# An FFT feeding a routed expert layer: loads, folds and the opening chain put in another order

## The chip, the cores and the metric

One core of a Trainium2 chip runs the whole program. The metric is the time of one execution on the device in microseconds (us), lower is better. A comparison gives the median of several executions of each kernel on the same chip.

## What is computed

```python
X = np.fft.fft(x, axis=1)          # x: 8 batches x 2496 rows x 256 columns
X = np.fft.fft(X, axis=2)
x = X.real.reshape(8 * 2496, 256)  # 19968 tokens
logits = x @ w_gate                # 8 experts
expert_idx = np.argmax(logits, axis=1)
gate_w = softmax(logits)[arange, expert_idx]
for e in range(8):                 # w1: 256 x 1024, w2: 1024 x 256
    out[mask_e] = gate_w[mask_e] * (relu(x[mask_e] @ w1[e]) @ w2[e])
```

## The kernel before

The work has two halves that overlap. The first half makes tokens: 16 units, each half of one batch's outputs (unit 2b is the even half of batch b, unit 2b+1 the odd half). The second half is the expert layer ("MoE"), which takes tokens of one expert in groups of 256 or 512 rows.

**Tokens.** A batch's rows arrive in the tile x, in four quarters and five slots of 128 rows. DVE folds them (`fold_w`, `fold_fg`, `fold_z`, `fold_h`, or `fold_half` for batch 1), so that symmetric rows are added and subtracted. TensorE then multiplies by cosine and sine tables cs0 (even half) and cs1 (odd half): `along_s(u, q)`, written (u, q) from here on, two chains of products per unit (q = 0 and 1), each ending in two PSUM banks; `s_out` copies one with ACT (tile ec) and lets DVE add and subtract into the tile pc or qc. `along_d(u)` multiplies five blocks of 128 columns by the tables in pack, ACT copies each result (tile pl) and DVE adds it into the unit's rows rb. `route_a` and `route_b` find each row's expert on DVE (lg, mx, ls, oh, mn, ohf, sm, then sc, rp, dst, di) and ACT (ex, sm, ohb); in their middle stand two small TensorE products with the triangle trib and the tile ones, which count the rows of each expert before a row. The result di is the row's place. `send` has GpSimd (POOL) scatter the unit's rows to the bucket in device memory, 10 indirect DMAs for a unit.

Column 0 of the second transform is a plain sum over all columns, which is made apart: `g1_fold` folds the tile xg on POOL, `g1_sums(par)` multiplies it by the tables, and `g1_rows(par, g1)` turns the 8 x 625 result so that it can be added to the rows (tile g1t).

**MoE.** When 2, 4, 7, 12 and 16 units are done, `group_table` makes a table on DVE that says which expert and which rows each of the next groups takes; SyncE (SP) loads it (`fetch`, tile row), reads registers from it, and loads weights (w1r, w2r) and rows (xr, L801). The first groups can only be loaded when the 20 scatters of units 0 and 1 have landed. A group then has its rows turned on TensorE (`xpose`, L852), split into a high and a low part (xh on ACT, xl on DVE), multiplied by split weights (wah, wal; L885 to L887), passed through relu (hh, hl), multiplied by the second weights (wb; L911, L912) and scattered to out.

**What sets the order.** Each engine runs its own instructions in the order in which they were built. The recorder places an instruction by readiness, and `with stage(engines)` ties all of a block's instructions on the named engines behind those of the block before. The opening (units 0 and 1 entire) is written out by hand in `fft_steps` as such blocks. From unit 2 on, the token work is a generator whose steps are taken a few at a time beside the steps of `moe_steps`; PRE of them are taken before the first MoE step.

The diff touches the opening's loads (L260 to L273), `stage`, `g1_sums`, `g1_rows`, `gate_weights`, `fold_first`, `route_a`, `along_d`, `fft_steps`, `xpose`, `gemm1` and `moe_steps`.

Of the kernel before, what the change touches and what calls it, by code (L numbers as in the profile page):

```python
# [21 lines left out]
P = 128  # L22
# [12 lines left out]
FSTEPS, PRE = (15, 26), 15  # L35
# [5 lines left out]
KEPT = 4  # L41
NE = NK * 2
# [152 lines left out]
def fft2_then_moe(ctx: ExitStack, tc: tile.TileContext, i: dict, out: bass.AP):  # L195
# [30 lines left out]
    def stage(*engines):  # L226
# [5 lines left out]
        for e in engines:  # L232
            mine = [q for q in traced[first:] if q.engine == e]
            for q in mine:
                for before in behind.get(e, ()):
# [3 lines left out]
            if mine:  # L239
                behind[e] = [q.name for q in mine]  # L240
# [27 lines left out]
    for t, n in ((pack, "c_pack"), (cdl, "c_cdl"), (wg, "wg"), (wgl, "wgl")):  # L268
        nc.sync.dma_start(out=t, in_=i[n])
    nc.sync.dma_start(out=cs0[:, 1], in_=i["c_cs0"][:, 1])  # L270
    load_x(1)
    nc.sync.dma_start(out=cs1[:, 1], in_=i["c_cs1"][:, 1])
    nc.sync.dma_start(out=ids, in_=i["c_ids"].rearrange("p (b n) -> p b n", b=B))  # L273
# [92 lines left out]
    def g1_sums(par):  # L366
        g1 = ff.tile([P, NKK], F32, name="pc")
        pe, po = bank("S"), bank("S")
        s_mm(pe, po, gz[:, par], gzs, par, B)
        ec = ff.tile([P, M], F32, name="ec")  # L370
        eo = ff.tile([P, M], F32, name="ec")
        nc.scalar.copy(ec[0:B], pe[0:B, 0:M])
        nc.scalar.copy(eo[0:B], po[0:B, 0:M])
        nc.gpsimd.tensor_add(g1[0:B, 0:M], ec[0:B], eo[0:B])
        nc.gpsimd.tensor_sub(g1[0:B, M : 2 * M - 1], ec[0:B, 0 : M - 1], eo[0:B, 0 : M - 1])
        return g1

    def g1_rows(par, g1):
# [11 lines left out]
    def gate_weights():  # L390
        nc.vector.tensor_copy(trib, tri)
        nc.vector.tensor_copy(tacc[:, 2:3], io[:, 2:3])
        nc.vector.tensor_add(wsum, wg[:, 0:E], wg[:, E : 2 * E])
        nc.vector.tensor_sub(wdif, wg[:, 0:E], wg[:, E : 2 * E])
        gp = bank("R")
# [75 lines left out]
    def fold_first():  # L471

        for sl in slots:
            yield from fold_w(0, sl)
            yield from fold_fg(0, sl)
            yield from fold_z(0, 0, sl, (0,))
            if sl is slots[1]:
                yield from fold_h(0, (0, 1))
# [99 lines left out]
    def fft_steps():  # L578
# [47 lines left out]
        with stage(PE, DVE):  # L626
            gate_weights()
# [453 lines left out]
```

## Time and profile before

| | us |
|---|---|
| median of 3 runs | 1107.19 |
| lowest, highest | 1101.07, 1109.17 |
| the profiled execution | 1100.43 |
| span of its instructions | 1098.4 |

The profile is of one execution. Its span goes from the first instruction to the last; 2.0 us of the execution's time lie around it. PE is TensorE's matmuls, PEld its weight loads, DVE is VectorE, ACT is ScalarE. A product of 32-bit operands has two records in the trace. PEclk is the granted TensorE clock as a share of full speed: 1.00 is 2.4 GHz, 0.50 is 1.2 GHz.

### The profile page before, as it was taken

Reading aid. Unit: us, or ns where it says so; the run is one execution under the profiler, and the core shown is the slowest. Engines: PE = TensorE matmul, PEld = TensorE weight load, DVE = VectorE, ACT = ScalarE, POOL = GpSimd, SP = SyncE. Lnnn points to the kernel's source line nnn. Section 1 sums busy time; section 2 is a strip of 40 time slices with the busy share of each in tenths; the row PEclk is TensorE's granted clock in tenths of the full one; section 3 lists DMA queues with packets and bytes.
Section 4 is the critical chain, followed back from the end, with each engine's and each line's share of the span. In section 5 each row is a group of like instructions: output and inputs, shape, how many; then the busy total and the mean of one; then the engine's idle time right before and its main releaser. Section 6 shows DMA issues by size and latency. Waiting matters only on the chain.

```text
span 1098.4 us, 19262 instructions
## 1 busy us (share of the span) xinstructions
PE 1071.3 (98%) x5840; PEld 897.1 (82%) x5840; DVE 817.3 (74%) x1819; ACT 582.3 (53%) x1330; POOL 358.9 (33%) x355
## 2 busy tenths in 40 slices
PE   8679999999999999999999999999999999999997
PEld 4459888898978878888887888888888888888896
DVE  6879997978897797976766776666766666666664
ACT  1347665566655545555555555555554455555554
POOL 2445433165155444533152552111211122111212
PEclk9679999999999999999999999999999999999999
DMA  9468667367886647655454556644564456544445
GB/s 366 171 225 296 231 228 265 119 223 223 278 219 198 212 110 238 173 158 154 116 164 121 160 172 173 165 116 116 166 159 137 116 149 159 154 116 128 161 175 195
DMA packets 185677, 197.88 MB, mean 180 GB/s; under 512 B 155515, under 2 KB 156316, under 8 KB 170844
## 3 DMA queue, kind: packets, MB, share of 16 engines
q1 hardware_dynamic: 170108, 154.06, 47.7%
q0 software_dynamic: 15456, 42.50, 10.3%
q8 instruction: 48, 0.79, 0.3%
q14 instruction: 65, 0.53, 0.1%
HBM read 154.03 MB, written 45.20 MB: 181 GB/s over the span
## 4 chain that ended last, share of the span: by engine, by line
PE 89%; issue 5%; DVE 2%; POOL 2%; DMA 2%; POOLq 0%; ACT 0%; SPq 0%; DVEq 0%; ACTq 0%
PE psY L911 26%; PE psH L885 13%; PE psY L912 13%; PE psH L886 13%; PE psH L887 13%; PE psH L318 6%; PE psH L598 2%; PE psH L599 1%; POOL bucket L549 1%; PE psY L318 1%; DMA x<-xin 1%; POOL out L920 1%; PE psH L852 1%; DMA bucket<-rb,di 0%; DMA xr<-bucket 0%
## 5 line engine op out<-in xcount | busy, mean ns | idle before, releaser
L911 PE MATMUL psY<-wb,hh 128*128 128x512 f32 x1296 | 474.4, 400 | 0.0
L912 PE MATMUL psY<-wb,hl 128*128 128x256 f32 x1296 | 363.1, 280 | 0.0
L920 POOL DMA_INDIRECT out<-ys,gt x162 | 170.4, 1052 | 539.1 <-DVE ys L919 502.3
L911 PEld LDWEIGHTS psY<-wb,hh 128*128 128x128 f32 x1296 | 243.5, 188 | 55.9 <-issue 2.2
L885 PE MATMUL psH<-xh,wah 128*128 128x512 f32 (+1 forms) x768 | 281.8, 367 | 0.7 <-ACT xh L854 0.7
L886 PE MATMUL psH<-xl,wah 128*128 128x512 f32 (+1 forms) x768 | 276.8, 360 | 0.2 <-DVE xl L855 0.2
L887 PE MATMUL psH<-xh,wal 128*128 128x512 f32 (+1 forms) x768 | 274.4, 357 | 0.0
L892 DVE SCALAR_TENSOR_TENSOR hl<-psH,hh 128x512 fp32r<-128x512 f32 x324 | 222.0, 685 | 47.3 <-ACT hh L891 43.5
L912 PEld LDWEIGHTS psY<-wb,hl 128*128 128x128 f32 x1296 | 244.6, 189 | 9.0
L861 DVE TENSOR_TENSOR wal<-w1r,wah 128x512 fp32r<-128x512 f32 x192 | 132.4, 690 | 153.7 <-ACT wah L860 150.1
L860 ACT CAST wah<-w1r 128x512 fp32r<-128x512 f32 x192 | 119.1, 621 | 213.7 <-PE psH L886 211.5
L891 ACT ACTIVATE hh<-psH 128x512 fp32r<-128x512 f32 x324 | 192.8, 595 | 65.6 <-PE psH L887 62.7
L549 POOL DMA_INDIRECT bucket<-rb,di x160 | 176.0, 1100 | 146.1 <-PE psH L887 59.7
L885 PEld LDWEIGHTS psH<-xh,wah 128*128 128x128 f32 x768 | 145.0, 189 | 29.3 <-issue 1.8
L887 PEld LDWEIGHTS psH<-xh,wal 128*128 128x128 f32 x768 | 145.5, 189 | 23.1
L886 PEld LDWEIGHTS psH<-xl,wah 128*128 128x128 f32 x768 | 145.5, 189 | 11.5 <-DVE xl L855 0.4
L871 ACT CAST wb<-w2r 128x512 fp32r<-128x512 f32 x192 | 119.9, 626 | 65.1 <-PE psY L912 61.7
L872 DVE TENSOR_TENSOR wb<-w2r,wb 128x512 fp32r<-128x512 f32 x192 | 130.8, 682 | 26.3 <-ACT wb L871 25.8
L854 ACT CAST xh<-psH 128x512 fp32r<-128x512 f32 x81 | 47.6, 590 | 46.7 <-DVE psH L848 45.1
L318 PE MATMUL psH<-cs,x 128*128 128x313 f32 (+3 forms) x336 | 71.7, 414 | 0.0
L919 DVE SCALAR_TENSOR_TENSOR ys<-psY,gt,ys 128x256 f32<-128x256 f32 x162 | 67.7, 474 | 3.2 <-ACT ys L918 3.2
L918 ACT ACTIVATE ys<-psY,gt 128x256 f32<-128x256 f32 x162 | 65.7, 481 | 4.3 <-PE psY L912 3.4
(144 smaller groups left out, 738.0 us busy)
## 6 DMA issues: line engine op xcount, KB each, us to landing
w1r<-w SPq DMA_DIRECT2D x50, 1024.0 KB, 5.4
w2r<-w SPq DMA_DIRECT2D x50, 1024.0 KB, 5.4
x<-xin SPq DMA_DIRECT2D x14, 1280.0 KB, 9.1
xr<-bucket SPq DMA_DIRECT2D x248, 64.0 KB, 4.8
xr<-bucket SPq DMA_DIRECT2D x15, 266.0 KB, 4.8
out<-ys,gt POOLq DMA_INDIRECT x162, 4.7
bucket<-rb,di POOLq DMA_INDIRECT x160, 4.5
bucket<-c_pad SPq DMA_DIRECT2D x8, 266.0 KB, 8.4
```

What stands on the lines that cost most here:

```text
L318: mm = lambda *a, **k: ch.update(pe=nc.tensor.matmul(*a, **k).ins)
L549: ins = nc.gpsimd.indirect_dma_start(out=bucket[:, :], out_offset=IndirectOffsetOnAxis(ap=di[:, n : n + 1].bitcast(U32), axis=0), in_=rb[: ...
L861: nc.vector.tensor_sub(lo, src, hi.bitcast(F32))
L872: nc.vector.tensor_sub(wb[:, :, 1], src, wb[:, :, 0].bitcast(F32))
L885: nc.tensor.matmul(o, lhsT=wh[:, c], rhs=xh[:, k, :], start=(k == 0), stop=False)
L886: nc.tensor.matmul(o, lhsT=wh[:, c], rhs=xl[:, k, :], start=False, stop=False)
L887: ins = nc.tensor.matmul(o, lhsT=wl[:, c], rhs=xh[:, k, :], start=False, stop=(k == 1))
L891: nc.scalar.activation(hh, hp, AF.Relu)
L892: nc.vector.scalar_tensor_tensor(out=hl, in0=hp, scalar=0.0, in1=hh.bitcast(F32), op0=ALU.max, op1=ALU.subtract)
L911: nc.tensor.matmul(y, lhsT=hh[:, c], rhs=wide_w, start=(first and q == 0), stop=end, skip_group_check=True)
L912: nc.tensor.matmul(y[:, 0:D], lhsT=hl[:, c], rhs=wb[:, f, 0], start=False, stop=end, skip_group_check=True)
L920: ins = nc.gpsimd.indirect_dma_start(out=out, out_offset=IndirectOffsetOnAxis(ap=gt[:, a, 1:2].bitcast(U32), axis=0), in_=ys, in_offset=No ...
```

## The change

Five things are done. The loads of the opening stand in another order. DVE folds batch 1 behind the first table, instead of during units 0 and 1, and the folds of batches 2 and 6, which stood beside units 3 and 11, now stand at units 4 and 12, behind the tables that follow units 3 and 11 (batch 2's also behind a named instruction of the second MoE group, `hold`). `g1_rows` adds column 0's two partial sums on TensorE: ten products that accumulate in pairs take the place of five transposes, POOL's adds go, and ACT makes four copies a half instead of two. `g1_sums(1)` and `g1_rows(1)` move from the start of the opening behind `along_d(0)`. The stages of the opening now tie PE, ACT and DVE, not mostly DVE alone. Smaller edits: the gate columns of a group are copied after its rows are turned, the copy of 127 columns in rb stands behind lg, seven of the eight pad loads come later, and the pace of the token steps is counted by `fft_work`.

```diff
     load_x0(slots[0])
     nc.sync.dma_start(out=xg, in_=i["xg"])
+    load_x0(slots[1])
     nc.sync.dma_start(out=cs0[:, 0], in_=i["c_cs0"][:, 0])
-    load_x0(slots[1])
-    nc.sync.dma_start(out=cs1[:, 0], in_=i["c_cs1"][:, 0])
     load_x0(slots[2])
...
     def g1_sums(par):
-        g1 = ff.tile([P, NKK], F32, name="pc")
         pe, po = bank("S"), bank("S")
         s_mm(pe, po, gz[:, par], gzs, par, B)
...
+        eo = []
+        for o, sign in ((pe, 1.0), (po, -1.0)):
+            t = ff.tile([P, NKK], F32, name="pc" if o is pe else "qc")
+            nc.scalar.copy(t[0:B, 0:M], o[0:B, 0:M])
+            nc.scalar.mul(t[0:B, M : 2 * M - 1], o[0:B, 0 : M - 1], sign)
+            eo.append(t)
+        return eo
...
         for kt in range(NK):
-            nc.tensor.transpose(out=gp[:, kt * B : (kt + 1) * B], in_=g1[0:B, KO[kt] : KO[kt] + P], identity=ident[0:B, 0:B])
+            for n, t in enumerate(eo):
+                nc.tensor.matmul(
+                    gp[:, kt * B : (kt + 1) * B], lhsT=t[0:B, KO[kt] : KO[kt] + P], rhs=ident[0:B, 0:B], start=(n == 0), stop=(n == 1)
+                )
...
-        g2 = g1_sums(1)
         with stage(PE, DVE):
-            run(fold_first())
+            for sl in slots:
+                run(fold_first(sl))
             along_s(0, 0, False)
         with stage(PE, DVE):
+            gate_sums()
+            run(fold_z(0, 1))
+            along_s(0, 1, False)
+        with stage(PE, ACT, DVE):
+            along_s_out(0, 0)
             gate_weights()
...
             g1_rows(0, g1)
...
             gate_g1(0)
...
+        with stage(PE, ACT, DVE):
             along_s_out(0, 1)
+            along_s(1, 0, False)
+        with stage(PE, ACT, DVE):
+            run(along_d(0))
+            g1 = g1_sums(1)
+            g1_rows(1, g1)
+            along_s(1, 1, False)
+        st, rb = {}, cols.pop(0)
+        with stage(ACT, DVE):
+            nc.vector.tensor_copy(trib, tri)
+            run(route_a(0, 0, rb, st))
+            along_s_out(1, 0)
             gate_g1(1)
...
+            along_s_out(1, 1)
+        with stage(PE, ACT, DVE):
             run(route_b(0, 0, rb, st))
             send()
...
+        load_x(2)
         ch["done"] = 2 if SEGS[0][0] == 2 else 0
+        yield
+        for h in (0, 2):
+            run(fold_half(1, h))
+        run(fold_z(1, 0))
+        run(fold_h(1))
```

Three places show what this does to the engines' order. The first is TensorE between unit 0's last transform and its first route product, before: the odd half's second chain (1, 1) in the banks psY_351 and psY_352, and right behind it the product with trib.

```order
L599 MATMUL psH<-pack,qc 128x136
L318 MATMUL psY_351<-cs_71,x 128x313 x2
L318 MATMUL psY_352<-cs_71,x 128x313 x2
L318 MATMUL psY_351<-cs_71,x 128x313
L318 MATMUL psY_352<-cs_71,x 128x313
L520 LDWEIGHTS trib
L520 MATMUL psH<-ohb,trib 128x80
```

The same place in the changed kernel; gz is the folded column-0 input, and the two L382 rows stand for five such pairs.

```order
L601 MATMUL psH<-pack,qc 128x136
L319 MATMUL psY_299<-cs_71,gz 8x313 x2
L319 MATMUL psY_300<-cs_71,gz 8x313 x2
L319 MATMUL psY_299<-cs_71,gz 8x313
L319 MATMUL psY_300<-cs_71,gz 8x313
L382 MATMUL psH<-pack,pc 128x8
L382 MATMUL psH<-pack,qc 128x8
...
L319 MATMUL psY_326<-cs_71,x 128x313 x3
L319 MATMUL psY_327<-cs_71,x 128x313 x3
L522 LDWEIGHTS trib
L522 MATMUL psH<-ohb,trib 128x80
```

The odd half's sums of column 0 and the ten products that turn them now stand in front of (1, 1) and of the route product. The second place is DVE in the changed kernel, from the end of the first table (tab) on; x is batch 1's tile.

```order
L760 TENSOR_SCALAR tab<-tacc 128x1
L761 TENSOR_TENSOR tab<-tacc 128x1
L457 TENSOR_TENSOR x<-x 128x1280 x2
L459 TENSOR_TENSOR x<-x 128x5x128
L461 TENSOR_TENSOR x<-x 128x5x128
L459 TENSOR_TENSOR x<-x 128x5x128
L461 TENSOR_TENSOR x<-x 128x5x128
L435 TENSOR_TENSOR x<-x 128x5x128 x3
L446 TENSOR_TENSOR zs<-x 128x512
L435 TENSOR_TENSOR x<-x 128x5x128
L448 TENSOR_TENSOR x<-x 128x2x2x128
```

These twelve folds were spread over units 0 and 1 and are now in one block behind the table, in front of everything that unit 2 needs. The third place is TensorE around the first MoE group, before: unit 3's second chain (six products with cs_71) stands in front of the turn of the first rows (xr).

```order
L520 MATMUL psH<-ohb,trib 128x80
L521 LDWEIGHTS ones
L521 MATMUL psH<-ohb,ones 128x80
L318 MATMUL psH<-cs_71,x 128x313 x6
L852 MATMUL psH<-pack,xr 128x128 x4
L885 MATMUL psH<-xh,wah 128x256 x2
```

And in the changed kernel:

```order
L522 MATMUL psH<-ohb,trib 128x80
L523 LDWEIGHTS ones
L523 MATMUL psH<-ohb,ones 128x80
L847 MATMUL psH<-pack,xr 128x128 x4
L885 MATMUL psH<-xh,wah 128x256
L319 MATMUL psH<-cs_71,x 128x313 x3
L886 MATMUL psH<-xl,wah 128x256
```

The turn of the first rows still stands behind unit 2's route products, while unit 3's second chain moved behind it, among the first group's products.

## Rows read from the trace of the kernel before

**Rows 1.** The page, part 1: busy us (share of the span) and instructions.

```profile
PE 1071.3 (98%) x5840; PEld 897.1 (82%) x5840; DVE 817.3 (74%) x1819; ACT 582.3 (53%) x1330; POOL 358.9 (33%) x355
```

**Rows 2.** Stretches: us, PE, PEld, DVE, ACT, POOL busy (instructions), PEclk, DMA share, GB/s.

```profile
0.00:81.00 81.00, 61.20 (x272) 39.78 (x273) 61.51 (x182) 23.70 (x88) 30.46 (x41) 0.77 0.69 255
81.00:1091.00 1010.00, 1009.90 (x5570) 857.30 (x5569) 754.86 (x1636) 558.17 (x1241) 326.49 (x313) 1.00 0.58 175
8.00:12.00 4.00, 1.17 (x10) 0.41 (x10) 2.05 (x4) 0.00 (x0) 2.77 (x7) 1.00 1.03 399
...
48.80:59.60 10.80, 10.80 (x43) 8.26 (x43) 8.97 (x42) 1.07 (x3) 8.39 (x10) 0.50 0.28 100
...
76.90:80.10 3.20, 2.98 (x14) 2.90 (x14) 2.65 (x5) 0.36 (x1) 0.00 (x0) 0.50 1.00 392
116.00:160.00 44.00, 43.90 (x300) 37.73 (x299) 42.01 (x143) 27.10 (x70) 18.68 (x18) 1.00 0.63 223
```

**Rows 3.** Timeline of PE: start us, us, line, operation, out<-in, records.

```profile
17.39 0.80 PE L318 MATMUL psY<-cs,x 128*128 128x156 f32 x4
...
20.15 0.39 PE L396 MATMUL psH<-wsum,pack 128*128 128x8 f32 x2
...
21.42 0.80 PE L318 MATMUL psY<-cs,zs 128*128 128x156 f32 x4
...
23.81 0.78 PE L381 MATMUL psH<-pack,pc 8*128 8x8 f32 x10
...
26.49 1.20 PE L598 MATMUL psH<-pack,pc 128*128 128x137 f32 x8
...
30.90 3.00 PE L318 MATMUL psY<-cs,x 128*128 128x313 f32 x12
37.02 0.22 PE L520 MATMUL psH<-ohb,trib 128*128 128x80 bf16 x1 [3.12 <-ACT ohb L505]
...
48.73 0.23 PE L520 MATMUL psH<-ohb,trib 128*128 128x80 bf16 x1 [5.25 <-ACT ohb L505]
...
48.83 2.20 PE L318 MATMUL psH<-cs,x 128*128 128x156 f32 x8
...
57.46 1.74 PE L598 MATMUL psH<-pack,pc 128*128 128x137 f32 x6
...
67.70 5.86 PE L318 MATMUL psH<-cs,x 128*128 128x313 f32 x12
...
76.48 0.50 PE L885 MATMUL psH<-xh,wah 128*128 128x256 f32 x2 [0.67 <-ACT xh L854]
```

**Rows 4.** Timeline of PE's weight loads.

```profile
20.15 0.30 PEld L396 LDWEIGHTS psH<-wsum,pack 128*128 128x128 f32 x2 [0.17 <-issue]
```

**Rows 5.** Timeline of DVE.

```profile
23.07 1.48 DVE L455 TENSOR_TENSOR x<-x 128x1280 f32<-128x1280 f32 x1
...
25.65 0.82 DVE L457 TENSOR_TENSOR x<-x 128x640 f32<-128x640 f32 x1
...
39.30 0.17 DVE L538 TENSOR_TENSOR di<-dst,pack 128x10 int32<-128x10 f32 x1
...
46.72 0.23 DVE L485 TENSOR_TENSOR lg<-rb,gg 128x80 f32<-128x80 f32 x1
...
50.63 0.17 DVE L538 TENSOR_TENSOR di<-dst,pack 128x10 int32<-128x10 f32 x1
...
56.99 0.14 DVE L761 TENSOR_TENSOR tab<-tacc 128x1 int32<-128x1 f32 x1
...
63.91 0.24 DVE L485 TENSOR_TENSOR lg<-rb,gg 128x80 f32<-128x80 f32 x1
```

**Rows 6.** Timeline of POOL: the first and the last of units 0 and 1's 20 scatters.

```profile
40.41 1.54 POOL L549 DMA_INDIRECT bucket<-rb,di  x1 [5.10 <-DVE x L457]
...
66.63 0.98 POOL L549 DMA_INDIRECT bucket<-rb,di  x1 [0.30 <-issue]
```

**Rows 7.** The chain that ended last, in order of time: the first load of rows.

```profile
72.28 2.76 DMA xr<-bucket
```

More of the change, by code (lines that the diff above doesn't have):

```diff
@@ L234, in stage @@
             for q in mine:
-                for before in behind.get(e, ()):
+                for before in [since] if since else behind.get(e, ()):
                     tc.add_manual_dep(
@@ L238, in stage @@
                     )
-            if mine:
+            if mine and not since:
                 behind[e] = [q.name for q in mine]
@@ L648, in fft_steps @@
-        rest = fold_half(1, 2)
-        with stage(DVE):
-            run(along_d(0))
-            run(half)
-            next(rest)
-        st, rb = {}, cols.pop(0)
-        with stage(DVE):
-            along_s(1, 0)
-            run(route_a(0, 0, rb, st))
-        with stage(DVE):
-            along_s(1, 1)
+            along_s(1, 0, False)
[4 more added lines that the diff above has]
+            along_s(1, 1, False)
@@ L668, in fft_steps @@
-        with stage(DVE):
+        with stage(PE, ACT, DVE):
+            nc.vector.tensor_copy(tacc[:, 2:3], io[:, 2:3])
             run(route(1))
             send()
+        load_x(2)
+        ch["done"] = 2 if SEGS[0][0] == 2 else 0
         yield
-        ch["done"] = 2 if SEGS[0][0] == 2 else 0
+        for h in (0, 2):
+            run(fold_half(1, h))
+        run(fold_z(1, 0))
+        run(fold_h(1))
         late = None
@@ L678, in fft_steps @@
                 pads(range(1, E))
-            if par == 0 and b + 1 < B:
+            if par == 0 and 1 < b < B - 1:
                 load_x(b + 1)
+            if par == 0 and u in NS and u > 2:
+                folds = fold_batch(b)
+                while True:
+                    with stage(DVE, since=ch.get("hold")):
+                        if next(folds, 0) == 0:
+                            break
+                    yield
             if (u, 0) not in cols:
@@ L689, in fft_steps @@
                 yield from fold_z(b, 1)
-            elif b + 1 < B:
-                with tc.issue_after(ch["tab"]) if b == 1 else nullcontext():
-                    yield from fold_batch(b + 1)
+            elif b + 1 < B and u + 1 not in NS:
+                yield from fold_batch(b + 1)
             yield from along_d(u)
             late = route(u)
-            if u + 1 in [n for n, _, _ in SEGS]:
+            if u + 1 in NS:
                 if par == 0:
@@ L855, in xpose @@
         nc.vector.tensor_sub(xl, hp, xh.bitcast(F32))
+        if part == 0 and not blocked(g):
+            gt = mo.tile([P, 4, 2], F32, name="gt", bufs=8)
+            nc.scalar.copy(gt[:, 0:n, 0], xr[:, 0:n, GATE])
+            nc.vector.tensor_copy(gt[:, 0:n, 1].bitcast(I32), xr[:, 0:n, TID].bitcast(I32))
+            ch[g, "gt"] = gt
     def split(src, name):
@@ L995, in fft_until, with fft_work @@
             yield
+    def fft_work(u):
+        folds = 19 if (u + 1) // 2 <= EARLY else 13
+        if u % 2:
+            return 13 + folds * (u + 1 not in NS)
+        return 15 + folds * (u in NS and u > 2)
     segs = cuts()
@@ L1027, in fft2_then_moe @@
         todo = fft_until(n)
-        rate = sum(FSTEPS[u % 2] for u in range(was, n))
+        rate = sum(fft_work(u) for u in range(was, n))
         if made[-2] == 0:
@@ L1042, in fft2_then_moe @@
                 next(todo, None)
-            with nullcontext() if k else stage(ACT, DVE):
+            with stage(ACT, DVE) if k < 6 else nullcontext():
                 next(moe)
```

81 lines of the change are left out of this document (26 added, 55 removed).

## The prediction

> **What bounds the kernel now.** I read the page first: TensorE is busy 98% of the span [rows 1]. A table of stretches then says where the other 2% lie [rows 2]. From 81 to 1091 us PE is busy 1009.9 of 1010 us at the full clock: no stall is left there that an edit could remove, and whatever stands outside it adds to the time one for one. From 0 to 81 us it is busy 61.2 of 81 us, at 0.77 of the clock. So all the edits must be judged by two numbers: when the first MoE product starts, and how much token work TensorE has done by then, because work that is left over costs its full length later.
>
> Before, the first MoE product (L885) starts at 76.48 [rows 3]. It hangs on the scatters: unit 0's places di are ready at 39.47, the first of 20 scatters starts at 40.41 and the last at 66.63 [rows 5, 6]; SP can issue the load of rows at 72.28, it takes 2.76 us [rows 7], and turning and splitting takes the rest. In the shadow of the scatters TensorE does unit 2 entirely and both chains of unit 3; the last of these runs from 67.70 to 73.56 [rows 3].
>
> **The opening, step by step.** Start: cs0's first half (128x939 numbers, 0.48 MB) now stands behind the second third of x; at 399 GB/s [rows 2] that is 1.2 us for x. I let (0,0) start 1.0 us earlier, 16.4 instead of 17.39. From there TensorE is one queue. (0,0) and what waits in it took 17.39 to 20.15, 2.8 us; the gate products 20.15 to 21.42, 1.3; (0,1) 21.42 to 23.81, 2.4 [rows 3]. So 22.9 so far.
>
> New: ten products for column 0 in place of five transposes. Before, ten transposes (both halves) took 23.81 to 24.52, 0.07 us each [rows 3]. A 32-bit product with 8 columns is priced by the gate's four: 1.27/4 = 0.32 us each. From below, the two weight loads of one such product end 0.30 us after the first begins, and the row's x2 covers one load of about 0.19 after a step of about 0.11 [rows 4], so 0.23 us each if nothing else counts. I take 0.25, near the loads, since the ten have no waits between them: 2.5 us a half (ends: 0.7 at the transposes' price, 3.2). That gives 25.4. (1,0) costs 3.0 like the chain at 30.90 [rows 3]: 28.4. `along_d(0)`: eight records of L598 took 26.49 to 27.53 and the other factor's as much, so 0.52 a block, 2.6 for five: 31.0.
>
> Now the moved part. `g1_sums(1)` used to run while TensorE waited for x; here it stands in the queue. Its six products are as wide as the chain at 30.90, 3.0 us: 34.0. Two ACT copies must follow before the ten products, some 0.7 us: 34.7. The ten products: 37.2. (1,1): 40.2. Then comes the route product, at 40.2 instead of 37.02. What is given back is the 3.12 us in which PE waited for ohb [rows 3]: `route_a` now hides behind this queue, so that cover is worth all it can be and is used up. ACT runs in order too: ohb, unit 0's, stands behind the four copies and the g1t copy, about 38.5, still before 40.2.
>
> di of unit 0: 2.45 us behind the route product before (37.02 to 39.47), plus about 0.4 because the adds of (1,1) now lie between: 43.05, that is 3.6 us later. The block scattering is not faster, so its end moves by the same. POOL loses two adds of 8 rows in each half, which lay in its idle time: nothing.
>
> Unit 1: ten adds on DVE (2.1 us) and lg at 45.4, then 4.1 us to di as before (46.72 to 50.80) [rows 5]: 49.5, 1.3 us earlier, because DVE has no folds among it. This gains nothing by itself: scatters 11 to 20 queue behind the first ten.
>
> The table took 50.80 to 57.13 with three folds and other adds in it; alone I take 4.2: 53.7. Then the twelve folds of batch 1: two of 1.48, eight of 0.82, two of about 0.7 [rows 5], less the overlap of neighbours, 10.5 us: 64.2. Before, unit 2's first chain started at 48.83; now TensorE has nothing between unit 1's route product (47.4) and 64.2. It comes back from a long idle, and there the row is plain: from 48.80 to 59.60 it was busy without a gap at 0.50 of the clock, 1.2 GHz [rows 2]. So I charge the chains of unit 2 as before, 48.83 to 57.46, 8.6 us: 72.8. From there to lg took 57.46 to 63.91, 6.45 us, with about 1 us of folds in it: 78.2. lg to the route product 2.0 us (46.72 to 48.73 [rows 3, 5]), plus 0.4 for an evacuation in front of it on ACT: 80.6.
>
> The order puts the turn of the first rows behind this product. Rows are there at about 79 (66.63 to 75.04 before, plus 3.6 to 4), so the token chain binds, not the scatters. Turn and split took 75.18 to 76.48, 1.3 us; two weight casts now stand in front of xh on ACT, 0.9: first MoE product at 82.9, 6.4 later.
>
> Against that: TensorE has been busy since 64.2, so the first products should run at the full clock, where before 2.98 us of them ran at half [rows 2]: 1.5 back. The wait for xl is filled by three products of (3,1): 0.7 back. But (3,1) itself, hidden before, is now on the path: 3.0 us. Sum: 6.4 - 1.5 - 0.7 + 3.0 = +7.2 us.
>
> The other edits come to nothing while PE has no stall: gate columns copied later, the copy behind lg, pads at unit 8 (0.27 MB each beside a DMA share near 0.6), the pace of the steps. Their cover is that same full PE queue; the second rival says what happens if it is gone.
>
> Of the profiled execution's own 1100.43 us (span 1098.4 and 2.0 around it) this makes 1107.6; that execution lies 0.6% below the median of the runs shown, so in the median's terms 1107.19 + 7 = 1114.
>
> **A rule on the clock.** The stretch 48.80 to 59.60 shows TensorE without a gap for 10.8 us and still at 1.2 GHz, while 76.9 to 80.1 took 3.2 us to be released [rows 2]. The Trainium skill, page TensorE: Matmul & The Clock Gate, section What's actually happening, says that activity releases the throttle after at least one busy window. By that rule the chains of unit 2 would run mostly at full speed; by the long row they don't. I follow the row of the same products; the other case is the first rival.
>
> **Rivals.** One: the clock comes back early. If unit 2's chains see it after 3.2 us, as the MoE products did, they take 3.2 us for 1.6 of work and 2.7 more, 5.9 instead of 8.6. The token chain then ends 2.7 us earlier, and the scatters (79) bind about as much: first product at 80.6 or so, +4.7 in all, 1112. With the column-0 products at the transposes' price as well, both halves save 3.6 and the sum is +1, 1108. For it: full activity. Against it: the row of just these products.
>
> Two, the slower one: DVE becomes the bound beside the MoE. Batch 2's folds cost about what batch 1's do, 10.5 us, and DVE did some two thirds of them, 7 us, in gaps of the opening before 76.48; now all stand beside MoE groups, tied behind the second group's first hl. From 116 to 160 us DVE is busy 42.0 of 44 us [rows 2], so at most 2 us of such a stretch are free. From the point at which DVE's queue falls behind by more than the three buffers of wal and wb, PE waits for it; if these 7 us find no room, 1114 + 7 = 1121. Against it: PE did not wait at 95%, and over 81 to 1091 us DVE has 255 us free.
>
> Three, the opening gains as its order suggests: ohb in time, no folds on DVE between, column 0 nearly free. Even then di of unit 0 cannot come before about 35, the twenty scatters take 26 and the load 9 more, and (3,1) is still owed: about -3, 1104.
>
> **How the numbers follow.** One per cent is 11 us, about what a measurement of this kernel can tell from no change. The forecast, 1114, has 0.52; rival one (1108 to 1112) 0.22; rival two (1121) 0.19; rival three 0.07. Only rival two passes +11 us, with a part of the forecast's own spread (a low clock already at 17 us, since PE idles longer there, adds up to 3): slower 0.20. Faster by 11 us needs more than rival three gives: 0.05. The range 1103 to 1122 reaches from rival three to rival two; the forecast's own is 1108 to 1119.
>
> **What would show it.** In the changed profile: the first L522 near 40 and not before 37; each half's ten L382 products in about 2.5 us; the first scatter near 43 to 44; no TensorE work from about 48 to 64; the first group's L885 near 83 with the clock at 1.00; and from there PE without a gap. If L885 comes before 76, the queue argument is wrong; if the stretch after 85 us shows PE waiting for wal, wb or hl, rival two holds.

## The result, and the profile after

The changed kernel took 1121.38 us (median of 6 runs, 1116.93 to 1126.11), the kernel before 1109.11 (6 runs, 1101.07 to 1110.49): ratio 1.0121, 95% interval 1.0082 to 1.016, slower by 12 us. The profiled execution took 1120.56 us, its span is 1118.7, 20.3 more than before; but before's profiled execution lies 8.7 us under its own median, so some 8 of the 20.3 belong to the pair of executions.

| us from the span's start | before | forecast | after |
|---|---|---|---|
| (0, 0) starts | 17.39 | 16.4 | 15.89 |
| (1, 1) starts | 30.90 | 37.2 | 39.30 |
| unit 0's route product | 37.02 | 40.2 | 46.74 |
| unit 1's route product | 48.73 | 47.4 | 54.64 |
| unit 2's first chain | 48.83 | 64.2 | 70.35 |
| first MoE product | 76.48 | 82.9 | 89.53 |

PE's timeline of the changed kernel, against [rows 3] (start, us, line, operation, records, the idle time before and who ended it):

```profile
15.89 1.26 PE L319 MATMUL psY<-cs,x 128*128 128x156 f32 x8
...
20.68 0.39 PE L398 MATMUL psH<-wsum,pack 128*128 128x8 f32 x2
...
21.94 0.38 PE L382 MATMUL psH<-pack,pc 8*128 8x8 f32 x2
...
24.27 4.74 PE L319 MATMUL psY<-cs,x 128*128 128x313 f32 x12
28.93 0.50 PE L600 MATMUL psH<-pack,pc 128*128 128x137 f32 x2
...
31.57 2.91 PE L319 MATMUL psY<-cs,gz 128*8 128x313 f32 x12
34.97 0.39 PE L382 MATMUL psH<-pack,pc 8*128 8x8 f32 x2 [0.49 <-ACT pc L373]
...
39.30 7.51 PE L319 MATMUL psY<-cs,x 128*128 128x313 f32 x12 [1.54 <-ACT ec L348]
46.74 0.25 PE L522 MATMUL psH<-ohb,trib 128*128 128x80 bf16 x1
...
54.64 0.22 PE L522 MATMUL psH<-ohb,trib 128*128 128x80 bf16 x1 [3.64 <-ACT ohb L507]
...
70.35 2.20 PE L319 MATMUL psH<-cs,x 128*128 128x156 f32 x8 [15.42 <-issue]
...
89.53 0.39 PE L885 MATMUL psH<-xh,wah 128*128 128x256 f32 x1 [1.34 <-ACT xh L849]
```

The same six products of 313 columns took 3.00 us before [rows 3]; here (1, 0) took 4.66 (24.27 to 28.93) and (1, 1) 7.44, after a wait of 1.54. The stretches say why (us, PE, PEld, DVE, ACT, POOL busy, clock, DMA share, GB/s):

```profile
23.00:25.00 2.00, 2.00 (x15) 1.83 (x16) 0.40 (x1) 0.52 (x2) 0.00 (x0) 1.00 0.97 400
25.00:27.00 2.00, 2.00 (x7) 1.23 (x5) 0.88 (x3) 0.00 (x0) 0.00 (x0) 0.62 0.12 41
27.00:29.00 2.00, 2.00 (x7) 0.58 (x5) 0.00 (x0) 0.00 (x0) 0.00 (x0) 0.53 0.00 0
29.00:31.00 2.00, 2.00 (x18) 1.96 (x17) 0.72 (x4) 0.99 (x7) 0.00 (x0) 1.00 0.00 0
...
39.00:41.00 2.00, 1.70 (x3) 1.17 (x4) 0.99 (x4) 0.45 (x2) 0.00 (x0) 0.53 0.00 0
41.00:43.00 2.00, 2.00 (x4) 0.50 (x2) 0.00 (x0) 0.00 (x0) 0.00 (x0) 0.50 0.00 0
```

Before, the chain at 30.90 ran at the full clock:

```profile
31.00:33.00 2.00, 2.00 (x9) 1.23 (x7) 1.78 (x6) 0.60 (x5) 0.00 (x0) 1.00 0.00 0
```

In the changed kernel TensorE was busy without a gap from 15.9, and its clock still fell to 1.2 GHz at about 25.5, 1.2 us into (1, 0), which follows 3.6 us of products of 8 columns (gate and column 0, 20.68 to 24.27). It fell again at about 39, within the wait in front of (1, 1). The wait of 1.54 us is read on ACT:

```profile
37.80 0.19 ACT L385 COPY g1t<-psH 128x40 f32<-128x40 f32 x1 [1.94 <-PE psH L382]
37.88 0.73 ACT L487 COPY rb<-rb 128x635 f32<-128x635 f32 x1
...
38.83 0.42 ACT L348 COPY ec<-psY 128x313 f32<-128x313 f32 x1
```

(1, 1) uses the banks of (1, 0), done at 28.93. ACT takes them over at 38.83 only, because the new order puts that copy behind g1t and `route_a`.

The first MoE products started at the full clock and lost it after 0.8 us, until about 93.7:

```profile
90.00:92.00 2.00, 2.00 (x7) 1.35 (x5) 1.69 (x6) 0.09 (x1) 0.00 (x0) 0.58 0.02 8
```

Beside the MoE, PE is busy 1015.4 of 1020 us from 92 to 1112 us, where before it idled 0.1 us in 1010 [rows 2]. Four waits make up 3.5 of these 4.6 us (in total, times, longest):

```profile
PE psH L885 <- DVE xl L850: 1.2, 1, 1.2
PE psY L913 <- DVE wb L872: 1.1, 1, 1.1
PE psY L914 <- DVE hl L892: 0.7, 1, 0.7
PE psY L913 <- ACT hh L891: 0.5, 1, 0.5
```

### The profile page after: what moved, and what is told of

The parts are those of the page before. It is cut to its first block, busy times and chain, and to the rows that moved or that the text cites. A ratio compares the mean times of both kernels' runs of the same rounds, so it can differ in the third digit from the quotient of the medians.

```text
span 1118.7 us, 19281 instructions
## 1 busy us (share of the span) xinstructions
PE 1078.0 (96%) x5870; PEld 902.2 (81%) x5870; DVE 814.1 (73%) x1819; ACT 582.6 (52%) x1334; POOL 358.4 (32%) x351
## 4 chain that ended last, share of the span: by engine, by line
PE 86%; issue 6%; DVE 5%; POOL 1%; DMA 1%; ACT 1%; POOLq 0%; SPq 0%; DVEq 0%; ACTq 0%
PE psY L913 24%; PE psH L885 13%; PE psY L914 12%; PE psH L886 12%; PE psH L887 12%; PE psH L319 7%; PE psH L600 2%; PE psH L601 2%; PE psY L319 2%; POOL out L922 1%; DMA x<-xin 1%; DVE hl L892 1%; DVE wal L861 1%; PE psH L847 0%; DVE x L435 0%
## 5 line engine op out<-in xcount | busy, mean ns | idle before, releaser
L922 POOL DMA_INDIRECT out<-ys,gt x162 | 173.0, 1068 | 493.1 <-DVE ys L921 456.9
L885 PE MATMUL psH<-xh,wah 128*128 128x512 f32 (+1 forms) x768 | 282.5, 368 | 2.5 <-ACT xh L849 1.3
L551 POOL DMA_INDIRECT bucket<-rb,di x160 | 173.6, 1085 | 171.9 <-PE psH L887 72.0
L885 PEld LDWEIGHTS psH<-xh,wah 128*128 128x128 f32 x768 | 144.9, 189 | 31.7 <-issue 2.1
L886 PEld LDWEIGHTS psH<-xl,wah 128*128 128x128 f32 x768 | 145.3, 189 | 11.2 <-DVE wal L861 0.2
L319 PE MATMUL psH<-cs,x 128*128 128x313 f32 (+3 forms) x336 | 69.9, 405 | 15.4 <-issue 15.4
L319 PEld LDWEIGHTS psH<-cs,x 128*128 128x128 f32 (+1 forms) x336 | 43.3, 197 | 35.4 <-issue 28.4
```

Source lines behind the costliest of these rows:

```text
L319: mm = lambda *a, **k: ch.update(pe=nc.tensor.matmul(*a, **k).ins)
L551: ins = nc.gpsimd.indirect_dma_start(out=bucket[:, :], out_offset=IndirectOffsetOnAxis(ap=di[:, n : n + 1].bitcast(U32), axis=0), in_=rb[: ...
L885: nc.tensor.matmul(o, lhsT=wh[:, c], rhs=xh[:, k, :], start=(k == 0), stop=False)
L886: nc.tensor.matmul(o, lhsT=wh[:, c], rhs=xl[:, k, :], start=False, stop=False)
L922: ins = nc.gpsimd.indirect_dma_start(out=out, out_offset=IndirectOffsetOnAxis(ap=gt[:, a, 1:2].bitcast(U32), axis=0), in_=ys, in_offset=No ...
```

## The experiments

They ran in five groups, each on another chip than the first result. There all kernels took some 3% longer (before 1138 to 1151 us by group), so each ratio is to before on the same chip, and places in a trace are compared within a group where that can be. A change of 0.3% is at the edge of what they tell. "L885" below is the first MoE product, whatever its line.

**The bank wait (e_evac).** `along_s_out(1, 0)` stands behind `along_d(0)`:

```diff
             run(along_d(0))
+            along_s_out(1, 0)
             g1 = g1_sums(1)
...
             run(route_a(0, 0, rb, st))
-            along_s_out(1, 0)
```

> The changed kernel (profiled span 1118.7 us), with one edit: the evacuation of (1, 0) stands right behind along_d(0), in front of the column-0 copies and of route_a. Queue theory (TensorE's queue in front of unit 0's route product was longer than forecast because (1, 1) waited 1.54 us for its banks and then ran 7.51 us at the low clock): no wait for ec, (1, 1) starts near 37.7, the route product L522 comes at 41 to 43 instead of 46.74, the first scatter near 45 to 47 instead of 50.41, and the first MoE product L885 4 to 5.5 us earlier, near 84 to 85.5; time 4 to 5.5 us less. If the gap alone let the clock fall, (1, 1) takes 3.0 us; if the ten narrow products in front of it did, it stays at 6 us or more. Rival (the token chain behind the folds of batch 1 sets L885 whatever the opening does): L885 moves by under 1 us only if the table, which hangs on unit 1's places, does not come earlier; the table at 60.36 must then stay too.

Ratio 1.0008 (0.9965 to 1.005). The wait for ec is gone, the route products came at 44.62 and 52.89, L885 at 87.42, although (1, 0) took 5.89 us at the low clock. (1, 1) began at the full clock, fell to 0.50 at 42.3 with no gap ahead of it since 37.9, and took 6.4 us with the narrow products among it. So the gap alone does not explain the clock:

```profile
41.00:42.00 1.00, 1.00 (x8) 0.91 (x8) 0.09 (x1) 0.32 (x2) 0.00 (x0) 1.00 0.00 0
42.00:43.00 1.00, 1.00 (x4) 0.36 (x2) 0.64 (x2) 0.84 (x4) 0.20 (x1) 0.66 0.00 0
43.00:44.00 1.00, 1.00 (x5) 0.51 (x4) 0.22 (x1) 0.27 (x1) 0.00 (x0) 0.50 0.00 0
```

The time cannot be told from that of the changed kernel, which had 1.0042 (1.0011 to 1.0073) in the next group.

**Column 0 on POOL again (e_transposes).** `g1_sums` and `g1_rows` as before, in the new places.

> The changed kernel, with column 0 added on POOL and turned by five transposes a half, as before the change, in the new places. Narrow-product theory (the ten products of 8 columns let TensorE's clock fall right behind them, at 25 and again at 39): without them (1, 0) runs at clock 1.00 and takes 3.0 us instead of 4.66, and the queue up to along_d(0) ends about 3 us earlier (transposes 0.35 us a half instead of 2.3, and 1.6 from the clock). In the second half POOL's two adds and their handovers, about 1.5 to 2 us, stand in the queue in place of the ten products, so L522 comes 3 to 6 us earlier than 46.74, and so does L885 (89.53); time 3 to 5 us less. Rival (the clock falls for another reason, such as the lull of the loads at 25): (1, 0) stays near 4.7 us, and only some 2 us are gained.

Ratio 0.9994 (0.9947 to 1.004); route products at 44.56 and 52.80, L885 at 87.39. The transposes gave the 2 us of their length. But the clock fell all the same, at 22.9, and (1, 0) took 4.72 us: there the gate's four products and five transposes, 1.7 us together, stood in front of it.

```profile
22.00:23.00 1.00, 1.00 (x8) 0.86 (x8) 0.29 (x1) 0.82 (x5) 0.00 (x0) 0.94 1.00 420
23.00:24.00 1.00, 1.00 (x3) 0.67 (x2) 0.99 (x3) 0.00 (x0) 0.00 (x0) 0.50 1.00 420
```

The ten products are not needed for the fall.

**The folds back in units 0 and 1 (e_folds).**

```diff
             along_s(1, 0, False)
+            run(fold_half(1, 0))
...
             run(route_a(0, 0, rb, st))
+            run(fold_half(1, 2))
             along_s_out(1, 0)
             gate_g1(1)
+            run(fold_z(1, 0))
+            run(fold_h(1))
             along_s_out(1, 1)
```

> The changed kernel, with the folds of batch 1 back inside units 0 and 1, in DVE's idle stretches (half 0 ahead of along_d(0), half 1 behind route_a, the rest ahead of the evacuation of (1, 1)). Token-chain theory (the folds behind the first table hold TensorE from 54.7 to 70.35 and so set L885): unit 2's chains start near 55, TensorE does not idle there, the chain of unit 2 ends some 10 us earlier, and then the scatters (last at 77.2) bind: rows at about 83, the turn and split 1.3 to 2 us more, so L885 at 84.5 to 87 instead of 89.53, and the chains of unit 3, which were partly left over, are done before it: in all 4 to 7 us less. Rival (the scatters bind already): L885 at 89 to 90 as now, and 0 to 3 us less, from the chains of unit 3 alone.

Ratio 1.0054 (1.0016 to 1.0091), L885 at 90.71: a miss. The folds delay the evacuations (a wait of 2.10 us inside (1, 1)), and unit 2, which does start at 57.43, then stands still:

```profile
76.75 0.42 ACT L348 COPY ec<-psH 128x313 f32<-128x313 f32 x1 [14.49 <-remote]
```

That copy needs only the chain (2, 1), which ended at 66.1. DVE stood still as well, until 79.66, 2.5 us past the end of that copy. What held the two is not in the profile.

**The old pace of the later folds (e_pace).** The folds of batches 2 and 6 and the constants of the pace as before.

> The changed kernel, with the folds of batches 2 and 6 beside units 3 and 11 as before the change (those of batch 2 behind the table), and the old pace of the token steps. Stall theory (the folds and steps that were moved make DVE late beside the MoE: five waits of 0.5 to 1.3 us on xl, wb, hl and hh, 4.6 us of TensorE idle between 92 and 1112): these waits go, the opening and L885 stay at 89.5, and the time falls by 3 to 4.5 us. Rival (the waits come from the token work that was left over when the MoE began): they stay, or others take their place, and the time moves by under 1.5 us.

Ratio 1.0135 (1.0058 to 1.0213), from four runs. Inconclusive for the waits: with the old pace the adds of unit 3's first chain stand on DVE in front of unit 2's routing (mx at 95.90), L885 comes at 104.39, and what follows is shifted. Beside the MoE, from 110 to 1090 us, PE idles 28.3 us, more than any other kernel of the study.

**Unit 0's route product moved up (c_after, e_route).** The control is the changed kernel. In the other, `route_a` and `route_b` of unit 0 stand ahead of the evacuation of (1, 0), the turning of the odd half's column 0 and (1, 1); `g1_sums` is cut in two for that, products and copies.

```diff
             run(along_d(0))
-            g1 = g1_sums(1)
-            g1_rows(1, g1)
-            along_s(1, 1, False)
+            banks = g1_mm(1)
...
             run(route_b(0, 0, rb, st))
             send()
+        with stage(PE, ACT, DVE):
+            along_s_out(1, 0)
+            g1_rows(1, g1_out(*banks))
+            along_s(1, 1, False)
```

> The changed kernel itself, once more, so that its variants are compared with it on the chip of this group, where kernels may run at other times than on the first chip. Every theory: its ratio to the kernel before is that of the first result, 1.008 to 1.016; the first route product near 46 to 50 and the first MoE product near 88 to 93.

> The changed kernel, with unit 0's route_a and route_b moved ahead of the evacuation of (1, 0), the turning of the odd half's column 0 and (1, 1); on TensorE the route product then stands right behind the six products of g1_sums(1). Queue theory (the first route product at 46.74 instead of 37.02 is what was lost, because everything of unit 1 stood in front of it): L522 becomes L528, near 35 to 37, the first scatter near 39 to 41 instead of 50.41, 10 us earlier. Unit 1's route product and the table hang on (1, 1), which is not moved up, so they come only 0 to 3 us earlier, and the folds of batch 1 behind the table then set the first MoE product: 85 to 89 instead of 89.53; time 1 to 4 us less than the changed kernel. Rival (the scatters alone set it): the first MoE product near 79, 10 us less.

The control: 1.0042 (1.0011 to 1.0073), route products at 49.47 and 57.37, L885 at 91.19. With the edit: 1.0034 (0.9996 to 1.0073), and on PE:

```profile
38.32 0.20 PE L528 MATMUL psH<-ohb,trib 128*128 128x80 bf16 x1 [0.66 <-ACT ohb L513]
...
54.68 0.22 PE L528 MATMUL psH<-ohb,trib 128*128 128x80 bf16 x1 [6.04 <-DVE ohf L509]
70.59 2.20 PE L319 MATMUL psH<-cs,x 128*128 128x156 f32 x8 [15.63 <-issue]
...
89.61 0.39 PE L893 MATMUL psH<-xh,wah 128*128 128x256 f32 x1 [1.34 <-ACT xh L857]
```

Unit 0's product came 11.2 us earlier than in the control and the last scatter 9.6 (70.31 against 79.95), but L885 only 1.6. It follows unit 1's product: by 34.9 us here, 34.9 in the first result, 33.8 in the control, 34.5 and 34.6 in the first two experiments. The scatters do not set it; the table, the folds and unit 2 do.

**Both (e_route_folds).** That edit with the folds of the third experiment.

> The edit of the run before it, and the folds of batch 1 back inside units 0 and 1 as well. Two-path theory (the scatters, which hang on unit 0's route product, and the token chain, which hangs on the table and the folds, both set the first MoE product, so that one moved alone gives 2 to 4 us and both give the sum and more): the first scatter near 40, TensorE without the long idle before unit 2, the first MoE product at 76 to 80 instead of 89.53, time 8 to 12 us less than the changed kernel, about that of the kernel before. Rival (one path alone sets it): no more than the better of the two edits alone.

Ratio 1.0002 (0.9965 to 1.0039), L885 at 92.00 in the profile: a fold on DVE in front of `route_a` held the first route product until 46.10, and the second came at 66.71. The two paths were not freed together, so this decides nothing.

**Before, with the folds behind the table (b_fold).** The twelve folds go from the stages of units 0 and 1 to where the changed kernel has them; nothing else changes.

> The kernel before, with one part of the change alone: the twelve folds of batch 1 stand behind the first table. Two-path theory: the first scatter stays near 40 and unit 0's route product near 37 or up to 3 us earlier, since DVE has no folds in its way; the table comes some 2 to 4 us earlier than 57, the folds end near 64 to 66, unit 2's chains start there instead of at 48.83, and the first MoE product comes at 80 to 83 instead of 76.48; time 4 to 8 us more than before. Rival (the folds' place costs nothing, since the scatters set the first MoE product): 76 to 77, no more than 1.5 us of difference.

Ratio 1.003 (0.9993 to 1.0066):

```profile
33.10 0.20 PE L520 MATMUL psH<-ohb,trib 128*128 128x80 bf16 x1 [0.30 <-ACT ohb L505]
...
40.95 0.22 PE L520 MATMUL psH<-ohb,trib 128*128 128x80 bf16 x1 [4.02 <-ACT ohb L505]
56.66 2.20 PE L318 MATMUL psH<-cs,x 128*128 128x156 f32 x8 [15.42 <-issue]
...
83.52 0.58 PE L877 MATMUL psH<-xh,wah 128*128 128x256 f32 x1 [0.67 <-ACT xh L846]
```

Freed of the folds, and with the clock at 1.00 from 16 to 38, the old opening has its route products 16.4 us ahead of the control's. L885 gains less, 7.7 us, since without the later edits three casts stand on ACT in front of unit 2's first evacuation (60.51 to 62.17) and unit 2's routing stands on DVE behind a fold of batch 2 that waits 6.52 us for its load. The time gains less still: the median, 1149.92, lies 2.0 us below the control's 1151.94, and beside the MoE (110 to 1090 us) TensorE idles 2.7 us more. So L885 alone does not give the time.

**The changed kernel with the old opening (x_open), and single parts put back.** x_open has before's loads, column 0 and stages, without the folds in them; the folds behind the table and all later edits stay. x_loads adds the new order of loads. x_tadd adds a second product, with zeros, to each transpose (`fprev` is zero there):

```diff
-            nc.tensor.transpose(out=gp[:, kt * B : (kt + 1) * B], in_=g1[0:B, KO[kt] : KO[kt] + P], identity=ident[0:B, 0:B])
+            for n, r in enumerate((ident[0:B, 0:B], fprev[0:B])):
+                nc.tensor.matmul(
+                    gp[:, kt * B : (kt + 1) * B], lhsT=g1[0:B, KO[kt] : KO[kt] + P], rhs=r, start=(n == 0), stop=(n == 1)
+                )
```

x_spin adds 55 idle products behind unit 1's route product:

```diff
+        with stage(PE):
+            wp = ps.tile([P, 512], F32, name="psH", bufs=4)
+            for q in range(55):
+                nc.tensor.matmul(wp, lhsT=trib, rhs=ones.unsqueeze(1).to_broadcast([P, 4, P]), start=True, stop=True)
```

> The changed kernel, with its whole opening (loads, column 0, order of the stages) as in the kernel before, but still without folds of batch 1 in it: these stay behind the first table, as changed, and so does everything after. Opening theory (in the changed kernel, and in its variant with unit 0's route product moved up, the first MoE product came 34.9 us behind unit 1's route product whatever unit 0's did, so what the change loses, it loses ahead of that product): as in the kernel before with the folds moved alone, unit 0's route product comes near 33.1 and unit 1's near 41, 13.7 us earlier than 54.64; the table near 46.5, unit 2's chains near 56.5, and the first MoE product at 41 + 34.9 = 76, instead of 89.5 and within 1 us of the kernel before; the time within 0.2% of the kernel before or better. Rival (the folds behind the table cost the 7 us that they cost in the kernel before): the first MoE product at 82 to 84.

> The run before it, with a second product behind each of the ten transposes of column 0, which adds zeros: ten products a half of 8 columns, as many as the changed kernel has, in the old place, and nothing else changed. Narrow-product theory (twenty products of 8 columns in a row take 0.223 us each and let TensorE's clock fall right behind them): they take 4.5 us instead of 0.7, the clock falls to 0.50 behind them, and unit 1's route product comes 4 to 8 us later than in that run; the first MoE product as much later. Rival (they cost their length alone, the clock stays at 1.00): 3 to 4 us later.

> The first kernel of this group, with the loads in the order of the changed kernel, and nothing else changed. Theory (the new order brings x earlier and the odd half's tables, the gate weights and the second batch later; only the new opening is written for it): (0, 0) starts up to 1.5 us earlier, but the products of column 0's odd half and (1, 0) wait for cs1, which lands near 25, so both route products come 2 to 6 us later. Rival (the order of the loads is free, TensorE's queue is what counts): both within 1 us of that run, or up to 1.5 us earlier.

> The first kernel of this group, with 55 idle products of 512 columns (16-bit, about 0.22 us each at the full clock) on TensorE behind unit 1's route product, where it waits 15.4 us for the table and the folds; they compute nothing that is used. Clock theory (unit 2's two chains take 8.6 us because TensorE comes back from the wait at 0.50 of the clock): the clock is back at 1.00 some 3 us after the first of them, unit 2's chains take 4.5 to 5 us, and the first MoE product comes 3.5 to 4.5 us earlier than in that run, at 71.5 to 73, unless the scatters hold it (their end was at 62 to 63, rows at 70 to 71). The time 3 to 4 us less than that run. Rival (the chains of 156 columns let the clock fall again, or the load of the rows binds): under 1.5 us.

| | ratio to before | route products | L885 |
|---|---|---|---|
| x_open | 0.9901 (0.9864 to 0.9938) | 39.47, 46.98 | 81.58 |
| x_tadd | 0.9998 (0.9968 to 1.0029) | 46.90, 54.41 | 88.17 |
| x_loads | 0.994 (0.9902 to 0.9977) | 42.02, 49.53 | 82.57 |
| x_spin | 0.9935 (0.9895 to 0.9974) | 38.28, 45.80 | 80.42 |

x_open is faster than the kernel before, though in its profile TensorE waited 2.07 us for the folds of x at 16.7, its clock was low from 20 to 34, and so its products came 6 us later than in b_fold; L885 is again 34.6 us behind the second. Two products for a transpose cost 9.7 us of the median and 6.6 of L885: 8.6 us in the queue (27.32 to 35.95) where ten transposes took 1.2, both at the low clock, so this run says nothing on whether they lower it. The loads cost 1.0 us of L885 and 3 us of the median, at the edge of the intervals. The idle products did not help:

```profile
52.00:60.00 8.00, 8.00 (x38) 3.63 (x37) 6.86 (x12) 0.00 (x0) 6.50 (x7) 1.00 0.31 90
60.00:64.00 4.00, 1.09 (x6) 0.49 (x5) 3.88 (x7) 0.00 (x0) 3.27 (x3) 1.00 0.97 306
64.00:66.00 2.00, 2.00 (x14) 1.35 (x14) 0.00 (x0) 0.00 (x0) 1.51 (x2) 0.85 1.01 409
66.00:72.00 6.00, 6.00 (x24) 4.41 (x25) 1.38 (x4) 0.84 (x2) 3.39 (x4) 0.50 0.47 178
```

The clock was at 1.00 when unit 2's chains began at 63.73, 2.91 us behind the last idle product, and fell 1.7 us into them.

**What the later edits and the odd half's place are worth (c_before, x_moe, x_move, x_first).** c_before is the kernel before, for its profile. x_moe is x_open with the folds in the opening, as before. x_move is x_open with `g1_rows(1, g1_sums(1))` behind `along_d(0)` and (1, 0), in front of (1, 1). x_first is x_open with the folds ahead of the table:

```diff
+        with stage(DVE):
+            for h in (0, 2):
+                run(fold_half(1, h))
+            for q in (0, 1):
+                run(fold_z(1, 0, ALL, (q,)))
+                run(fold_h(1, (q, q + 1)))
         load_x(2)
         ch["done"] = 2 if SEGS[0][0] == 2 else 0
         yield
-        for h in (0, 2):
-            run(fold_half(1, h))
-        run(fold_z(1, 0))
-        run(fold_h(1))
```

> The kernel before itself, profiled on the chip of this group, where the variants ran some 40 us longer than on the first chip. Every theory: ratio 1.00. Theory (this chip has waits of TensorE beside the MoE that the first one had not, and the later edits of the change remove some of them): from 120 to 1090 us TensorE idles by 20 us or more here, against 0.1 on the first chip, and the first MoE product is near 77 to 80. Rival (the opening is what differs between the chips): it idles as little as on the first chip, and the first MoE product is later than 85.

> The kernel before with the later edits of the change alone: the opening, its loads and its folds of batch 1 as before; the folds of batches 2 and 6 behind the tables, the early load of batch 2, the pace, the gate columns copied later and the stages of the first six MoE steps as changed. Theory (what made the changed kernel with the old opening 1% faster than before is these later edits): ratio to before 0.987 to 0.995. Rival (it is the folds of batch 1 behind the table, which free DVE in the opening): 0.997 to 1.003.

> The changed kernel with the old opening (0.9901 of before), and in it the odd half's sums of column 0 and their transposes moved behind along_d(0) and (1, 0), in front of (1, 1), as in the changed kernel; POOL's adds and the transposes stay. Queue theory (what stood in the shadow of x now stands in TensorE's queue, with its handovers, and the waits let the clock fall): unit 0's route product 4 to 8 us later than 39.5 minus what the earlier start of (0, 0) gives (3 us), and unit 1's and the first MoE product 2 to 6 us later; ratio to before 0.992 to 0.996. Rival (the place costs nothing, since (0, 0) starts as much earlier): within 1 us of that run.

> The changed kernel with the old opening, and the folds of batch 1 moved ahead of the first table, behind unit 1's places, quarter by quarter, so that unit 2's first chain needs only half of the last folds. Theory (the table is needed only when the weights are, the folds set the token chain): TensorE's wait in front of unit 2 falls from 15.6 to 10 us, unit 2's route product and the first MoE product come 4 to 5 us earlier; the weights land in time; ratio to before 0.985 to 0.988. Rival (the table's row, the weights and the load of the rows then bind): no gain, 0.990 or more.

| | ratio to before | route products | L885 |
|---|---|---|---|
| c_before | 0.9997 (0.9955 to 1.004) | 45.19, 56.90 | 91.73 |
| x_moe | 0.9999 (0.9966 to 1.0033) | 44.82, 56.41 | 87.11 |
| x_move | 1.0034 (1.0004 to 1.0063) | 45.60, 53.41 | 87.40 |
| x_first | 0.9973 (0.9939 to 1.0006) | 39.52, 47.03 | 82.41 |

The later edits alone give nothing, though L885 comes 4.6 us before c_before's. The odd half's place costs 0.6% against x_first (where the folds of batch 1 stand elsewhere too) and 5 to 6 us of L885: its transposes wait 1.72 and 0.52 us for POOL's adds in the middle of TensorE's queue. c_before suggests why the change costs 0.4% on the control's chip and 1.2% on the first, as far as one profile of each kernel, on two chips, can: here before's own opening was at the low clock from 20 to 37, its first MoE product is as late as the changed kernel's, and beside the MoE both idle alike (c_before in the opening; from 110 to 1090 us c_before and then the control):

```profile
22.00:32.00 10.00, 10.00 (x37) 6.60 (x36) 5.66 (x10) 1.11 (x6) 0.00 (x0) 0.50 0.79 313
```

```profile
110.00:1090.00 980.00, 958.85 (x5170) 806.61 (x5169) 711.68 (x1566) 522.48 (x1179) 306.44 (x295) 0.99 0.56 167
```

```profile
110.00:1090.00 980.00, 958.39 (x5153) 803.88 (x5151) 716.15 (x1572) 519.77 (x1162) 310.96 (x297) 0.99 0.56 169
```

Of the 43 us by which c_before's span exceeds that of the first chip's profile, 21 are this idle time and 15 the later first MoE product.

**The two fastest side by side (x_open2, x_first2).** The same two kernels, five rounds.

> The changed kernel with the old opening, once more, beside the next one. Theory: 0.990 to 0.997 of the kernel before. Rival (its 0.9901 came from the group that it ran in): 0.998 to 1.001.

> The same with the folds of batch 1 ahead of the table, once more, beside the one before it. Theory (the folds ahead of the table bring unit 2 forward by 5 us, but the weights then land beside the last scatters and the rows come 5 us later, so the first MoE product hardly moves): within 0.3% of the run before it. Rival: 0.3 to 0.6% less than that run.

0.993 (0.9903 to 0.9957) and 0.9919 (0.9888 to 0.995), medians 1138.74 and 1138.75 against 1146.83. Both beat the kernel before, and so the changed one, on these chips; neither ran on the first. Ahead of the table or behind it, the folds cost the same: x_first2 starts unit 2 3.7 us earlier than x_open2 (57.97 against 61.62), but its weights are loaded only beside the last scatters, and its load of rows starts 5.1 us later (76.70 against 71.58). In x_first the turn of these rows waits 3.95 us for them. In x_first2 it does not: there ACT stands still for 4.6 us behind (2, 1), and unit 2's route product comes 3.1 us later than in x_open2 (81.01 against 77.95).

## Why the prediction was wrong

The forecast was 1114 us, 7 more than before (1107.19 by the runs shown then); measured were 12 more (1121.38 against 1109.11). The frame held. TensorE's queue in front of the route products got longer, the token chain and not the scatters set the first MoE product (e_route shows it), unit 2's chains took 8.6 us at 1.2 GHz (70.35 to 78.97), the gate products 1.3, the ten products 2.3 of 2.5 forecast, `along_d(0)` 2.6, the folds 9.9 of 10.5. From unit 1's route product to the first MoE product the forecast had 35.5 us; it was 34.9. (0, 0) even started 0.5 us earlier than forecast.

The step that failed is "(1,0) costs 3.0 like the chain at 30.90" and, behind it, "The ten products: 37.2. (1,1): 40.2". The terms measured: (1, 0) 4.66 instead of 3.0; a wait of 1.54 for the banks that was not in the sum; (1, 1) 7.44 instead of 3.0. That is 7.6 us, against 6.5 by which unit 0's product and 7.2 by which unit 1's came later than forecast. Both prices were taken from a row at 2.4 GHz; here the clock was at 1.2. I had asked only whether the clock would be low after a long wait, not whether it could fall while TensorE is busy. Why it fell stays open: it fell without that wait in front of (1, 1) in e_evac, and without the ten products in e_transposes. And for the wait I looked at TensorE's order and not at who frees the banks: (1, 0)'s evacuation, listed in the change behind `route_a`. e_evac shows that part: the wait went, and the product came 2.1 us earlier than in the first result, 4.9 earlier than in the control.

Of the 13.05 us by which the first MoE product moved, 5.9 lie ahead of unit 1's route product, and 7.1 behind it (34.9 against 27.75): the folds, nearly as forecast (35.5). Of the 20.3 us between the two profiles, 13.05 are the move of the first MoE product and 4.5 the waits beside the MoE. The rest is 2.8, where the forecast had 0.8: the 1.5 us that the first MoE products were to give back did not come, since their clock fell at 90.3.

Rival two, DVE as the bound beside the MoE, was right in kind on the first chip, but smaller: TensorE idled 4.6 us from 92 us on, 3.0 of them for DVE, against the 7 priced. On the other chips the control idles no more than the kernel before. What these waits come from was not settled; e_pace, meant for it, changed too much.

Rival one did not come: the clock was 0.50 through unit 2's chains and on to 83.6, 13.2 us without a gap. In x_loads it did come, within 4 us (0.50 from 65 to 68, 0.88 from 68 to 72, 1.00 after). The Trainium skill, page TensorE: Matmul & The Clock Gate, section What's actually happening, says that activity releases the throttle, after at least one busy window: x_loads agrees, the 13.2 us of the changed kernel do not.

Rival three named what was there to gain, but not how: an opening without folds has its route products earlier (33.10 and 40.95 in b_fold), and the new order of the opening gives more than that back. The time falls only when the later edits come with it: moving the folds alone gave 1.003 (b_fold), the later edits alone 0.9999 (x_moe), both together 0.9901 and 0.993 (x_open, x_open2). Put back one at a time into x_open, the second product per transpose cost 1.0%, the odd half's place 0.6% (against x_first) and the loads 0.4%, while the opening as a whole costs 1.1 to 1.4% (0.9901 and 0.993 against the control's 1.0042, in different groups). The parts overlap.

One thing could not be seen in one profile: that of before was a lucky one, 1100.43 against a median of 1109.11, with the clock at 1.00 from 15.4 to 35. In c_before the same code was at 0.50 from 20 to 37.

## What to carry to other kernels

When instructions are put into a fixed order on several engines, follow each bank from its last product to the copy that frees it, on every engine's queue; a copy listed late stops TensorE as surely as a missing operand. Price a product from a row at the clock that will hold there, and at both clocks where that is not known: here the clock fell behind narrow products, behind short waits and in the midst of chains. Before moving work off a path, find which of two paths ends last: here 11 us off the scatters' path brought the first MoE product forward by 1.6, and what gained time was to take DVE's folds out of the opening, keep the later edits and leave the rest of the opening alone.

## What was not expected of the hardware

- TensorE's clock fell to 0.50 in the midst of work: at 25.5 in the changed kernel (no gap since 15.9), at 42.3 in e_evac (no gap since 37.9), at 65.4 in x_spin (1.7 us into a chain), at 90.3 in the changed kernel (0.8 us into the first MoE products). In the first two, products of 8 columns came just before. That these are the cause is argued, not shown: e_transposes, with fewer of them, fell too.
- A 32-bit product of 8 columns costs 0.22 us at 2.4 GHz and 0.43 at 1.2 (x_tadd), hardly less than one of 137 (0.23 at 2.4 GHz). The two weight loads fill that time: over the ten products from 21.94 to 24.27, PEld was busy 2.31 of 2.33 us.
- POOL's add of 16 columns took 1.27 us while DVE ran an instruction of 1.23 us; before, DVE stood idle then, and the add took 0.22. In six kernels in which the add began within a DVE instruction it ended 0.07 to 0.09 us after that instruction; in e_folds and e_pace, where it began up to 0.07 us ahead of DVE's, it took 0.22 and 0.21:

```profile
10.36 1.27 POOL L364 TENSOR_TENSOR gzs<-gz 128x16 f32<-128x16 f32 x1
10.33 1.23 DVE L420 TENSOR_TENSOR x<-x 128x1024 f32<-128x1024 f32 x1 [0.29 <-DMA x<-xin]
```

- On the other chips ACT stood still for 4 to 11 us behind the end of (2, 1), released by nothing that the profile names, in four kernels whose unit 2's chains ran within 57 to 67 us (c_before, x_moe, e_folds, x_first2). It stayed open; x_first, the same program as x_first2, and the kernels with the folds behind the table had no such gap.
